# Moving the third group's decay scans behind two mask operations on the vector engine

## The chip, the cores and the metric

One core of a Trainium2 chip runs the whole kernel. The metric is the device time of the program in microseconds (us), as the median of several runs. The engines are TensorE (PE in the rows: matmuls, and PEld its weight loads), VectorE (DVE), ScalarE (ACT), GpSimd (POOL) and SyncE (SP, which issues the transfers).

## What is computed

Two stages. The first is a linear recurrence over 768 time steps, for 32 pairs of batch and head, with a 40 x 40 state each:

```python
for t in range(S):
    y[:, :, t] = np.einsum('bhd,bhde->bhe', rt, state)
    Sa = np.einsum('bhde,bhe->bhd', state, at)
    state_decay = state * wt[:, :, None, :] - np.einsum('bhd,bhe->bhde', Sa, bt)
    state = state_decay + np.einsum('bhd,bhe->bhde', vt, kt)
```

The second stage takes the recurrence's output as a (4, 768, 320) tensor and runs four gated causal attention experts over it. The change touches only the first stage.

## The kernel before

The recurrence is cut into 24 chunks of 32 time steps, and these into 6 groups `W` = 0 to 5 of four chunks. For each group there is preparation, in two halves `a` = 0 and 1:

- `a` (L192): a suffix scan of the decays `w` on DVE, which writes `SUF`; `b` (L194, L195): a reciprocal into `D1P` and the chunk's total decay `PC`; `s` (L197): the prefix scan, which writes `SC`. `SC` needs `D1P` of the same half.
- `X` (L201): two products on POOL, `AB` = `EA` times `SC`. `K` and `H` (L205): two products each on POOL, which scale the keys `KB` by `SUF`.
- `f` and `g` (L189): checks of the decays' size on ACT.
- `m` (L226): 64 small matmuls per half, of `KB` with `AB`, into PSUM `pk`; DVE and POOL read them out as `GB` and `GK`. `L`, `t`, `T`, `P`, `B`, `D`, `Q`: the group's 32 x 32 triangular inverses.

The main loop takes steps `n` = 0 to 24. The table `MAIN` gives the parts of a step their order, ten places counted from 0: `g` of chunk n (L328, reads the state `ST` and `AB`), `f` of chunk n-1 (L342 on PE, then the mask multiplication of `FX` on DVE, L343), `t`, `u` (L333), `y` of chunk n-1 (L353 reads `FX`), `z`, `k` (L310), `s` (L373 on PE, then the new state `ST` on DVE; at a group's last chunk it is L364, L364 and L378, which multiply by `PC`), `w`, `v` (L324).

The work of the groups is hung between these places by strings, one for each step: `SIDE` for a group in general, `SIDE1` for group 1, with the parts of a string split at "/" standing behind places 0, 1, 2 and so on. Group `W` prepares itself in steps 4(W-1)-4 to 4(W-1)+3, so the third group, `W` = 2, has its string -2 in step 2, its -1 in step 3 and its 0 in step 4 (the third, fourth and fifth step). The kernel writes its order by hand: each engine executes its instructions in the order in which these parts were called, and waits on semaphores for what they read and for the buffers that they overwrite.

```python
    -2: "//l2/////l30f0g/0a0b0s",
    -1: "0X0K0H/1a1b/1e/////1K1H/1f1g1s1X",
    0: "///m0//////m1L",
```

Of the kernel before, what the change touches and what calls it, by code (L numbers as in the profile page):

```python
# [35 lines left out]
         (1, "0e0l0u1l1u1w1e"), (0, "o0"), (1, "0a0b0K0H"), (0, "i1 L B k0 x3 j47 t28 j0 j23 S o1 Z"), (1, "0f0g1f1g"), (0, "D"), (1, "0s1a0X1H"),  # L36
         (0, "P v0 Q"), (1, "1b1s"))

SIDE1 = ("////////n01p1xi0o0", "///n1i1o1L//Bt6//t8", "/t8//t6////T", "//P/D/////Q")


def layouts(r, k, v, w, a, b):
# [40 lines left out]
def recurrence(tc, ctx, I, xT, FL, CM, early, tail=None):  # L83
# [4 lines left out]
    V, A, T, PL, SY = nc.vector, nc.scalar, nc.tensor, nc.gpsimd, nc.sync  # L88
# [300 lines left out]
    def at(n, s, *fs):  # L389
        jobs.setdefault((n, s), []).extend(fs)  # L390

    def items(W, line, inv, td):

        fs, i = [], 0
        while i < len(line):
            x = line[i]
            if x == " ":
                i += 1
            elif x in "LTSZPQBD":
                fs.append(inv[x])  # L400
                i += 1
            elif x in "tj":
                j = i + 1
                while j < len(line) and line[j].isdigit():
                    j += 1
                m = int(line[i + 1:j])
                if x == "t":
                    fs += td[:m]
                    del td[:m]
                else:  # L410
                    fs.append(lambda m=m: busy(m))
                i = j
            else:
                y = line[i + 1]
                if x == "x":
                    fs.append(lambda y=y: fill(int(y)))
                elif x == "l":
                    fs.append(lambda y=y: load_k(W, int(y)))
                elif x == "c":
                    fs += [lambda k=k, y=y: load_c(int(y), k) for k in (range(4) if y == '0' else (1,))]  # L420
                elif x == "m":
                    fs.append(lambda y=y: mm(W, int(y)))
                elif x in "nio":
                    fs.append(lambda x=x, y=y: mm(W, int(y), x))
                elif x == "v":
                    fs.append(lambda y=y: units[int(y)]["v"]())
                elif x == "k":
                    fs.append(lambda y=y: keys(int(y)))
                else:
                    fs.append(preps[W, int(x)][y])  # L430
                i += 2
        return fs

    preps = {(w, a): prep(w, a) for w in range(NW) for a in range(2)}
    for W in range(1, NW):
        inv = invert(W)
        td = list(inv["t"])
        for r, line in SIDE.items():
            n = 4 * (W - 1) + r
            line = SIDE1[r] if W == 1 and r >= 0 else line  # L440
            for k, part in enumerate(line.split("/") if n >= 0 else ""):
                assert k < 10
                at(n, k, *items(W, part, inv, td))
        assert not td
# [406 lines left out]
def body(tc, I, out):  # L851
    with ExitStack() as ctx:
        dp = ctx.enter_context(tc.tile_pool(name="xd", bufs=1, space=DRAM))
        xT = dp.tile([4, 320, 768], F32, name="xT")
        fp = ctx.enter_context(tc.tile_pool(name="flag", bufs=1))
        FL = fp.tile([128, 24], F32, name="FL")
        CM = fp.tile([128, 261], F32, name="CM")
        FI = fp.tile([1, 1], I32, name="FI")
        with ExitStack() as c1:
            c1.enter_context(tc.manual_schedule())  # L860
            pre = []
            def tail(raw):
                p, jobs = prepare(tc.nc, ctx.enter_context(tc.tile_pool(name="pre", bufs=1, side="right", reuse_waits="tile")), I, xT, raw)
                pre.append(p)
                return jobs
            recurrence(tc, c1, I, xT, FL, CM, ExitStack(), tail)
        with ExitStack() as c2:
            moe(tc, c2, I, xT, out, CM[:, 0:128], pre[0], FL, FI)

        far = tc.nc.values_load(FI, min_val=0, max_val=1)  # L870
        with tc.If(far != 0):
            with ExitStack() as c3:
                c3.enter_context(tc.manual_schedule())
                step_by_step(tc, c3, I["RAW"], xT)
            with ExitStack() as c4:
                moe(tc, c4, I, xT, out, CM[:, 0:128], pre[0])
# [25 lines left out]
```

## Time and profile before

| | us |
|---|---|
| median of 3 runs | 609.68 |
| lowest, highest of them | 608.61, 610.55 |
| the profiled execution's own time | 608.79 |
| its span, first to last instruction | 607.0 |
| PE busy in the span | 566.0 (93%) |
| DVE busy | 475.9 (78%) |
| ACT busy | 364.2 (60%) |
| POOL busy | 257.3 (42%) |

The recurrence takes the first 345 us or so. The busy shares are means over two stages with different limits, so the place of the change has to be read by itself: steps 2 to 4 lie between 72 and 116 us.

### The profile page before, as it was taken

What the parts mean: (1) busy time and instruction counts of PE and PEld (TensorE: products, weight loads), DVE (VectorE), ACT (ScalarE), POOL (GpSimd) and SP (SyncE); (2) the same over time, 40 slices, a digit from 0 to 9 for tenths busy, and PEclk for the clock granted to TensorE, in tenths of its full rate; (3) what the DMA queues carried; (4) which work ended last, traced back from release to release, by engine and by line L of the source; (5) the groups of instructions that cost most, each with busy time, mean ns of one, the idle gap of its engine ahead of it and who ended that gap; (6) DMA issues with size and microseconds to landing.
All of it is one profiled execution on the core that took longest, in us unless ns stands there. A gap on an engine that the chain in (4) does not pass through costs nothing.

```text
span 607.0 us, 23642 instructions
## 1 busy us (share of the span) xinstructions
PE 566.0 (93%) x10111; PEld 496.1 (82%) x10111; DVE 475.9 (78%) x963; ACT 364.2 (60%) x740; POOL 257.3 (42%) x233
## 2 busy tenths in 40 slices
PE   7998999899999999999999879989999989999996
PEld 3547898899989989989999768878888878987884
DVE  8999899589498678766324369999989997898892
ACT  4854356367356456644546337757776777778873
POOL 5247309807914931960000232546544353333550
PEclk9999999999999999999999879989999999999998
DMA  6622352453354255223146244212311312020102
GB/s 153 176 89 57 119 150 69 119 143 117 94 162 123 78 145 148 67 71 97 49 138 159 55 115 117 53 50 68 84 43 45 82 36 70 24 53 11 56 2 72
DMA packets 44196, 54.09 MB, mean 89 GB/s; under 512 B 20098, under 2 KB 33666, under 8 KB 44082
## 3 DMA queue, kind: packets, MB, share of 16 engines
q1 hardware_dynamic: 43794, 52.32, 31.0%
q8 instruction: 82, 1.34, 0.9%
q10 hardware_dynamic: 288, 0.17, 0.2%
q14 instruction: 32, 0.26, 0.1%
HBM read 38.31 MB, written 7.86 MB: 76 GB/s over the span
## 4 chain that ended last, share of the span: by engine, by line
PE 60%; DVE 22%; DMA 6%; ACT 5%; issue 3%; POOL 2%; SPq 0%; DVEq 0%; ACTq 0%
PE pt L659 6%; PE ot L784 4%; PE pk L272 4%; PE sc L739 4%; PE ps L373 4%; PE pf L353 4%; PE pt L769 4%; PE pt L795 4%; PE pf L355 3%; PE pk L226 3%; PE pg L324 3%; PE pu L333 3%; PE pk L310 3%; PE pg L328 3%; PE pf L342 2%
## 5 line engine op out<-in xcount | busy, mean ns | idle before, releaser
L761 POOL TENSOR_TENSOR P<-P,m 128x128 f32<-128x128 f32 (+2 forms) x96 | 89.1, 950 | 116.5 <-DVE m L757 59.5
L201 POOL TENSOR_TENSOR AB<-EA,SC 40x1024 f32<-40x1024 f32 x18 | 48.9, 2714 | 83.5 <-PE pg L328 61.6
L750 ACT ACTIVATE P<-sc,m 128x128 f32<-128x128 f32 (+2 forms) x96 | 60.8, 634 | 25.5 <-DVE m L749 15.0
L784 PE MATMUL ot<-pt,vv 128*128 128x256 f32 (+1 forms) x384 | 61.1, 292 | 5.7 <-DVE ots L790 5.5
L739 PE MATMUL sc<-ks,qs 128*128 128x384 f32 (+4 forms) x256 | 62.3, 346 | 3.6 <-ACT P L750 2.9
L773 DVE TENSOR_TENSOR pt<-pt,pt 128x384 fp32r<-128x384 f32 (+1 forms) x96 | 59.0, 619 | 5.3 <-ACT pt L772 3.6
L784 PEld LDWEIGHTS ot<-pt,vv 128*128 128x128 f32 x384 | 51.5, 191 | 9.8 <-DVE ots L790 8.2
L749 DVE TENSOR_REDUCE m<-sc 128x1 f32<-128x128 f32 (+2 forms) x96 | 58.7, 615 | 0.9 <-PE sc L742 0.4
L772 ACT ACTIVATE pt<-pt 128x384 fp32r<-128x384 f32 (+1 forms) x96 | 51.9, 543 | 10.5 <-PE pt L769 9.0
L205 POOL TENSOR_TENSOR KB<-KB,SUF 104x512 f32<-104x512 f32 x38 | 57.0, 1534 | 0.9 <-DMA KB<-in_EK 0.5
L769 PE MATMUL pt<-CM,P 128*128 128x128 f32 x336 | 53.0, 275 | 3.8 <-DVE qs L668 2.6
L353 PE MATMUL pf<-FX,LS 128*40 128x64 f32 x768 | 47.7, 224 | 3.6 <-DVE FX L343 3.4
L353 PEld LDWEIGHTS pf<-FX,LS 128*40 128x40 f32 x768 | 42.3, 118 | 6.6 <-DVE FX L343 5.5
L659 PE MATMUL pt<-xh,wq 128*128 128x384 f32 x192 | 42.9, 359 | 4.7 <-DVE qs L668 4.5
L739 PEld LDWEIGHTS sc<-ks,qs 128*128 128x128 f32 x256 | 40.4, 191 | 7.4 <-ACT P L750 6.9
L355 PE MATMUL pf<-RX,SD 80*40 80x64 f32 x736 | 45.8, 222 | 0.0
L233 POOL TENSOR_TENSOR GK<-GK,CM 128x512 f32<-128x512 f32 x23 | 27.5, 1196 | 41.0 <-DVE GK L231 29.8
L335 ACT ACTIVATE R<-pu 32x640 f32<-32x640 f32 x48 | 33.3, 694 | 19.1 <-PE pu L333 18.5
L330 ACT ACTIVATE GT<-pg,CM 128x320 f32<-128x320 f32 x48 | 22.7, 523 | 36.3 <-PE pg L328 36.1
L343 DVE TENSOR_TENSOR FX<-pf,MK 128x1024 f32<-128x1024 f32 x24 | 29.1, 1213 | 18.6 <-PE pf L342 18.5
L769 PEld LDWEIGHTS pt<-CM,P 128*128 128x128 f32 x336 | 36.7, 141 | 7.4 <-issue 3.4
L355 PEld LDWEIGHTS pf<-RX,SD 80*40 80x40 f32 x736 | 41.6, 119 | 0.2 <-ACT SD L350 0.2
(152 smaller groups left out, 1367.4 us busy)
## 6 DMA issues: line engine op xcount, KB each, us to landing
ks<-ks SPq DMA_DIRECT2D x32, 192.0 KB
KB<-in_EK SPq DMA_DIRECT2D x32, 160.0 KB
EA<-in_EA SPq DMA_DIRECT2D x24, 160.0 KB
V<-in_V SPq DMA_DIRECT2D x24, 160.0 KB
R<-in_VX SPq DMA_DIRECT2D x48, 80.0 KB
RX<-in_RX SPq DMA_DIRECT2D x48, 80.0 KB
RB<-in_RB SPq DMA_DIRECT2D x48, 80.0 KB
xT<-XT SPq DMA_DIRECT2D x24, 160.0 KB
```

Of the source, the lines that this page charges most:

```text
L205: e.tensor_tensor(x, x, sv[:, :, 1:33].rearrange("p (x t c) n -> p x t c n", t=2, c=4)[:, :, t], op=OP.mult)
L353: T.matmul(pf[rows(r), x], ls[:, x, r], FX[:, :, x, r], start=True, stop=c == 0)
L355: T.matmul(pf[rows(r), x], SD[:, x, r], RX[:, :, x, r], start=False, stop=True)
L659: T.matmul(p, w, x, start=(j == 0), stop=(j == len(prs) - 1))
L739: T.matmul(ps[:, c, 0:cw], QS[b][:, e, o], KS[b][:, e, z, k], start=(z == 0), stop=(z == 1 and not last), skip_group_check=True)
L749: V.tensor_reduce(m[:, 0, t:t + 1], ps[:, 0:ch, 0:cw], axis=AX.XY, op=OP.max, negate=True)
L750: later(DE, lambda: A.activation(pv, ps[:, 0:ch, 0:cw], AF.Exp, bias=m[:, 0, t:t + 1], accum_out=m[:, 1, t:t + 1]))
L761: PL.tensor_tensor(P[:, 0:n], P[:, 0:n], m[:, 3, t:t + 1].to_broadcast([128, n]), op=OP.mult)
L769: T.transpose(p[:, 128 * y:128 * y + 128], st["P"][t][:, 128 * c:128 * c + 128], ident)
L772: A.activation(h, p[:, 0:n], AF.Copy)
L773: later(DL, lambda: V.tensor_tensor(l, p[:, 0:n], f32(h), op=OP.subtract))
L784: T.matmul(po[:, 128:256] if one else po, VV[b][:, k, e].rearrange("p a b -> p (a b)"), PT[:, 256 * k:256 * k + (128 if one else 256)], st ...
```

## The change

A second table of exceptions, `SIDE2`, gives group 2 strings of its own for steps 2, 3 and 4; `SIDE1` becomes a dictionary with the same content. The two scans of half 0 (`0a0b0s`) leave the end of step 2 (behind place 8) for step 3, behind place 1, that is behind the mask of `FX`; `0X0K0H` are written behind them instead of behind place 0. The last scan `1s` and the product `1X` leave the end of step 3 for step 4, behind place 1, again behind a mask of `FX`; `1K1H` are written at the end of step 3 instead of behind its place 7.

```diff
-SIDE1 = ("////////n01p1xi0o0", "///n1i1o1L//Bt6//t8", "/t8//t6////T", "//P/D/////Q")
+SIDE1 = {0: "////////n01p1xi0o0", 1: "///n1i1o1L//Bt6//t8", 2: "/t8//t6////T", 3: "//P/D/////Q"}
+
+SIDE2 = {-2: "//l2/////l30f0g", -1: "/0a0b0s0X0K0H1a1b/1e//////1f1g/1K1H", 0: "/1s1X//m0//////m1L"}
...
-            line = SIDE1[r] if W == 1 and r >= 0 else line
+            line = {1: SIDE1, 2: SIDE2}.get(W, {}).get(r, line)
```

On DVE, where step 2 ends and step 3 begins, before (`DD` is the last transpose of group 1's inverse, `SUF_86`, `D1P` and `SC_100` are half 0 of the third group, `SUF_87` its half 1; the lines are those of the kernel before):

```order
L259 STREAM_TRANSPOSE DD_90<-MT_89 128x16x32
L192 SCALAR_TENSOR_TENSOR SUF_86<-EW_84,D_83 104x1056
L194 RECIPROCAL D1P_88<-SUF_86 104x8
L195 TENSOR_TENSOR PC_97<-SUF_86 104x8
L197 SCALAR_TENSOR_TENSOR SC_100<-EW_84,D1P_88 104x1056
L343 TENSOR_TENSOR FX_117<-pf,MK 128x1024
L192 SCALAR_TENSOR_TENSOR SUF_87<-EW_85,D_83 104x1056
```

The same place of the changed kernel, whose lines below the tables are numbered higher by two:

```order
L261 STREAM_TRANSPOSE DD_90<-MT_89 128x16x32
L345 TENSOR_TENSOR FX_117<-pf,MK 128x1024
L194 SCALAR_TENSOR_TENSOR SUF_86<-EW_84,D_83 104x1056
L196 RECIPROCAL D1P_88<-SUF_86 104x8
L197 TENSOR_TENSOR PC_97<-SUF_86 104x8
L199 SCALAR_TENSOR_TENSOR SC_100<-EW_84,D1P_88 104x1056
L194 SCALAR_TENSOR_TENSOR SUF_87<-EW_85,D_83 104x1056
```

The mask has moved ahead of half 0's four instructions, and half 1's suffix scan now follows half 0's prefix scan directly.

On DVE, where step 3 ends and step 4 begins, before (`ps` is the state's update, `TT_110` the inverse that `u` reads, `pk` the result of `m0`):

```order
L364 TENSOR_TENSOR ps<-ps,PC_96 104x2x320
L378 TENSOR_TENSOR ST_118<-ST_118,ps 104x640
L281 TENSOR_TENSOR TT_110<-TT_110,pk 48x32x16 x2
L197 SCALAR_TENSOR_TENSOR SC_100<-EW_85,D1P_88 104x1056
L343 TENSOR_TENSOR FX_117<-pf,MK 128x1024
L229 TENSOR_TENSOR GB_105<-pk,CM 128x512
```

And in the changed kernel:

```order
L366 TENSOR_TENSOR ps<-ps,PC_96 104x2x320
L380 TENSOR_TENSOR ST_118<-ST_118,ps 104x640
L283 TENSOR_TENSOR TT_110<-TT_110,pk 48x32x16 x2
L345 TENSOR_TENSOR FX_117<-pf,MK 128x1024
L199 SCALAR_TENSOR_TENSOR SC_100<-EW_85,D1P_88 104x1056
L231 TENSOR_TENSOR GB_105<-pk,CM 128x512
```

Here the mask and half 1's prefix scan have changed places, and nothing else. On PE, ACT, POOL and SP the order of all instructions is the same in both kernels: the parts that were written elsewhere keep their rank among their engine's instructions.

## Rows read from the trace of the kernel before

**Rows 1.** Who waited for whom, PE, 60 to 122 us: total, times, longest

```profile
PE pk L226 <- POOL AB L201: 1.2, 1, 1.2
PE pf L353 <- DVE FX L343: 1.2, 2, 0.6
PE pg L328 <- DVE ST L380: 0.8, 1, 0.8
```

**Rows 2.** Timeline, PE, step 3: start, duration, engine line, [idle before <-releaser]

```profile
85.54 1.15 PE L342 MATMUL pf<-RB,VR 80*64 80x64 f32 x32 [0.17 <-ACT VR L339]
...
90.44 1.30 PE L333 MATMUL pu<-GT,TT 64*32 64x80 f32 x32
92.39 0.36 PE L353 MATMUL pf<-FX,LS 128*40 128x64 f32 x3 [0.65 <-DVE FX L343]
```

**Rows 3.** Timeline, DVE, steps 3 and 4

```profile
85.41 1.03 DVE L259 STREAM_TRANSPOSE DD<-MT 128x512 f32<-128x512 f32 x1
86.28 2.30 DVE L192 TENSOR_TENSOR_SCAN SUF<-EW,D 104x1056 f32<-104x1056 f32 x1
...
88.86 2.36 DVE L197 TENSOR_TENSOR_SCAN SC<-EW,D1P 104x1056 f32<-104x1056 f32 x1
91.13 1.20 DVE L343 TENSOR_TENSOR FX<-pf,MK 128x1024 f32<-128x1024 f32 x1
92.25 3.48 DVE L192 TENSOR_TENSOR_SCAN SUF<-EW,D 104x1056 f32<-104x1056 f32 x1
...
95.88 1.84 DVE L195 TENSOR_TENSOR PC<-SUF 104x8 f32<-104x8 f32 x1
...
99.83 0.82 DVE L378 TENSOR_TENSOR ST<-ST,ps 104x640 f32<-104x640 f32 x1
100.57 1.40 DVE L281 TENSOR_TENSOR TT<-TT,pk 48x512 f32<-48x512 f32 x2
102.00 3.18 DVE L197 TENSOR_TENSOR_SCAN SC<-EW,D1P 104x1056 f32<-104x1056 f32 x1
105.21 1.23 DVE L343 TENSOR_TENSOR FX<-pf,MK 128x1024 f32<-128x1024 f32 x1
```

**Rows 4.** Timeline, POOL, the third group's products

```profile
91.35 6.34 POOL L201 TENSOR_TENSOR AB<-EA,SC 40x1024 f32<-40x1024 f32 x2 [18.84 <-DMA EA<-in_EA]
97.77 11.84 POOL L205 TENSOR_TENSOR KB<-KB,SUF 104x512 f32<-104x512 f32 x8
109.57 4.41 POOL L201 TENSOR_TENSOR AB<-EA,SC 40x1024 f32<-40x1024 f32 x2
```

**Rows 5.** Timeline, PE, step 4

```profile
101.05 1.13 PE L328 MATMUL pg<-ST,AB 104*64 104x40 f32 x32
...
105.13 2.08 PE L226 MATMUL pk<-KB,AB 104*64 104x64 f32 x64
107.05 0.31 PE L353 MATMUL pf<-FX,LS 128*40 128x64 f32 x4
...
111.66 1.13 PE L324 MATMUL pg<-V,GK 64*64 64x40 f32 x32
114.03 2.09 PE L226 MATMUL pk<-KB,AB 104*64 104x64 f32 x64 [1.24 <-POOL AB L201]
```

**Rows 6.** Timeline, POOL, the same products of the fourth group

```profile
140.78 6.39 POOL L201 TENSOR_TENSOR AB<-EA,SC 40x1024 f32<-40x1024 f32 x2 [20.53 <-PE pg L328]
...
159.10 4.44 POOL L201 TENSOR_TENSOR AB<-EA,SC 40x1024 f32<-40x1024 f32 x2
```

**Rows 7.** Timeline, second group: POOL's products, DVE's scan beside them

```profile
50.61 6.30 POOL L201 TENSOR_TENSOR AB<-EA,SC 40x1024 f32<-40x1024 f32 x2 [2.35 <-ACT MT L276]
...
50.40 2.33 DVE L192 TENSOR_TENSOR_SCAN SUF<-EW,D 104x1056 f32<-104x1056 f32 x1
```

**Rows 8.** Timeline, PE, the fourth group's last matmuls of `m`

```profile
162.60 1.13 PE L324 MATMUL pg<-V,GK 64*64 64x40 f32 x32
163.66 2.08 PE L226 MATMUL pk<-KB,AB 104*64 104x64 f32 x64
```

**Rows 9.** Stretches: us, busy of PE, PEld, DVE, ACT, POOL, granted clock, DMA

```profile
112.80:114.00 1.20, 0.00 (x0) 0.00 (x0) 0.00 (x0) 0.02 (x1) 1.18 (x1) 1.00 0.57 143
114.00:116.00 2.00, 1.97 (x68) 1.97 (x68) 0.00 (x0) 0.00 (x0) 1.86 (x2) 1.00 0.64 183
...
352.00:356.00 4.00, 0.24 (x1) 0.27 (x2) 2.22 (x5) 0.10 (x2) 1.40 (x1) 0.78 0.92 238
356.00:360.00 4.00, 4.00 (x13) 4.00 (x14) 3.37 (x19) 1.18 (x3) 2.21 (x3) 0.50 0.05 12
```

## What the change should do to the time

> **What bounds the kernel now.** PE is busy for 93% of the span, so only a place where PE stands still can give time back, or take more. I read PE's waits in the stretch of the change first [rows 1]. They name three releasers: the mask of `FX` on DVE (twice, 1.2 us together), the `AB` products of POOL (1.24 us, once) and the state. Then the timelines of PE, DVE and POOL there. In step 3, PE finishes `f` at 86.69 (85.54 + 1.15) and `u` at 91.74, and then stands for 0.65 us until the mask is done [rows 2]. The mask's input was ready at 86.69, but DVE was in the two scans of half 0 until 91.22 and wrote the mask only from 91.13 to 92.33 [rows 3]. So the scans cost PE 0.65 us, and this is what the change can give back at most in that step. The second look goes to what the scans feed. POOL starts half 0's `AB` products at 91.35, 0.13 us after `SC` is done at 91.22 [rows 3, 4]. The row names a transfer as the releaser, but the wait has several semaphores and in the fourth group the same start names PE; the scan's end is what fits the time. From there POOL runs without a pause through two products of `AB`, eight of `KB` and two of `AB`, until 113.98 [rows 4]. At 114.03 PE starts the last 64 matmuls of `m` after an idle of 1.24 us, and that is POOL's end plus 0.05 [rows 5]. The reader should see that half 0's scans begin a chain (scan, POOL for 22.63 us, PE) that already ends last in step 4. PE's wait for the mask lies beside that chain, with 1.24 us of slack behind it.
>
> **The change, part by part.** No instruction is added or removed. Only DVE's order changes, at two places; the order of PE, ACT, POOL and SP stays, and so do the transfers that SP issues.
>
> Mask ahead of half 0's scans (step 3). The mask needs `pf` at 86.69; DVE is done with the transpose ahead of it at 86.44 (85.41 + 1.03) [rows 2, 3]. It starts near 86.7 and ends near 87.9, well ahead of `u`'s end, so PE's 0.65 us go, and PE is early by 0.65 us from there. What DVE pays: the first scan began at 86.28. It will now begin one mask later, 86.7 plus 1.12 (the distance of the mask's start from the next start, 91.13 to 92.25 [rows 3]), which is 87.82. That is 1.54 us later, of which 1.12 is the mask and the rest is idle time waiting for `pf`. Bounds: if the mask's start lags the matmuls by 0.1 us it is 1.65, and if it starts at the transpose's end it is 1.3. I take 1.55. Half 0's `SC` is then ready at 92.77 and POOL starts at 92.9.
>
> The chain on POOL. Its length in the third group is 22.63 us (91.35 to 113.98 [rows 4]) and in the fourth 22.76 (140.78 to 163.54 [rows 6]), though DVE's scans meet it at other moments there. The length contains time in which POOL and DVE hold each other up: the first pair of products takes 6.34, the last pair of the same form 4.41 [rows 4], and the scan beside the first pair takes 3.48 instead of 2.30 [rows 3]. In the changed order half 1's suffix scan follows half 0's prefix scan with no mask between, and starts just ahead of POOL. The second group has this order already: the scan starts at 50.40, POOL at 50.61, the scan takes 2.33 and the pair 6.30 [rows 7]. So the pair's length stays, between 6.30 and 6.39. The other meeting, with `1s` (3.18 instead of 2.36 [rows 3]), stays inside POOL's eight `KB` products, which will run from about 99.3 to 111.1. I take 22.63 again, with 22.5 to 22.8 as bounds. POOL ends at 115.5, and PE's `m` starts at 115.6 instead of 114.03: plus 1.55 us.
>
> The Trainium skill, SBUF — State Buffer, section "Who interferes with whom", says that a VectorE instruction with two SBUF inputs and a GpSimd instruction that reads SBUF exclude each other, the one that starts first holding the shared port to its end. By that rule the scan would run from 92.7 to 95.0 and the pair behind it for 4.4 us, to 99.4, where the row's 6.34 from 92.9 gives 99.24: the sum would be plus 1.7 instead of plus 1.55, and the time 611.4.
>
> What PE does until then. If nothing else moves, PE reaches `m` at 112.79 - 0.65 = 112.1. What can make it later is the state. Half 1's `PC` was held on DVE until POOL's pair was done (95.88 + 1.84 = 97.72), and behind it in DVE's queue stand the two multiplications by `PC` and the addition that ends at 100.65; PE's `g` of step 4 starts at 101.05 with no idle [rows 3, 5]. With the pair ending 1.55 us later the addition ends between about 100.3 (if `PC` gets in between the two products) and 102.3, so `g` starts between 100.4 and 102.4, up to 1.35 later than before. PE then reaches `m` between 112.1 and 114.15. Both lie ahead of 115.6, so this costs nothing in the sum; the cover is POOL's chain.
>
> `1s` behind the mask of step 4. Before, that mask ended at 106.44 and PE began `y` at 107.05 straight from `m0` [rows 3, 5], so there is nothing to win. What waits behind `1s` now: the read-out of `m0`, which PE's `k` needs, and half 1's `AB` products. The scan will start between 103.7 and 106.8, takes 2.4 to 3.5 us and is done by 110.3, while POOL gets to those products at about 111.1. `k` may be up to 1 us late; that lies in PE's slack of at least 1.4 us ahead of `m`. Cost: 0, with 0.5 as the upper bound if every delay falls together. `1K1H`, written two places later, have the same rank on POOL: 0.
>
> After `m` everything follows PE, or starts from what PE and DVE finish, so I find nothing that takes the delay back: in the fourth group POOL's chain ends at 163.54 and PE comes to its `m` at 163.66 [rows 6, 8], both started from the shifted work.
>
> Sum: plus 1.55 us. Against the profiled execution's own time it is 608.79 + 1.55 = 610.3; that execution lies 0.9 us under the median, so against the median 609.68 it is 611.2, plus 0.25%.
>
> **The rivals.** First, the gain stays. If the suffix scan and the first pair don't hold each other up in the new order, the pair takes 4.4 instead of 6.34, POOL ends at 113.6, and PE, which is there at 112.1, starts `m` at 113.65, 0.4 us earlier: 609.3. With more saved at the second meeting it could reach the 0.65 us, 609.0. It decides by the pair's length: under 4.8 us there is a gain. For it: the length does contain some 2 us of hold-up. Against it: the second group, with this very order, shows 6.30 [rows 7].
>
> Second, no change: the delay is there at 114 us and is made up later, at the hand-over between the stages, where PE was nearly idle from 352 to 356 us [rows 9]. It would need a stop there that does not come from the recurrence's last chunks. For it only that the rows there are dense with transfers; against it that these transfers bring the recurrence's own output. 609.7.
>
> Third, slower by more. PE would stand for up to 3.5 us ahead of `m` (112.1 to 115.6) instead of 1.24. After 1.2 idle us the granted clock stayed at 1.00, but after a stretch of 4 us with PE busy for 0.24 it was 0.50, the lower level of 1.2 GHz [rows 9]. If the clock fell here too, and the 4 us behind it ran at half speed, 2 us of work would be lost: 613.2. It decides by the idle time: if `g` waits for the state, PE arrives at 114 and the idle is 1.5 us, as before. Against it: the rows on both sides of the present wait are at 1.00.
>
> The Trainium skill, TensorE: Matmul & The Clock Gate, section "What's actually happening", has the lower level as the default that activity lifts, which is the mechanism of this rival; no row here has an idle time of just this length.
>
> **How the numbers follow.** A comparison of this kernel's runs can tell about 0.3%, 1.8 us, from no change. The forecast of 611.2 gets 0.62, with its own bounds 610.7 to 611.9; about a third of that lies over 0.3%. The gain gets 0.14, no change 0.13, the clock 0.11. Slower by over 0.3%: 0.62 / 3 + 0.11 = 0.32. Faster by over 0.3% needs more than any row offers; 0.06 for what I don't see. Within 0.3%: 0.62. The range of 609.2 to 612.6 leaves out most of the clock's case and part of the gain's.
>
> **What would show it.** Right: the mask of step 3 starts near 86.7 and PE has no wait for it; POOL's first pair starts near 92.9 and takes 6.3; PE's wait for `AB` ahead of `m` grows from 1.24 to between 1.4 and 3.5; `m` starts near 115.6, and all later rows are 1.5 us later. Wrong: a pair of 4.4 us, `m` at 114.0 or earlier, a granted clock under 1.00 after it, or a later stretch in which the difference shrinks. If half 0's scans start at 86.3 as before, the change did not do what it says.

## The result: slower by 0.6%

| | median, us | against the kernel before |
|---|---|---|
| before | 608.5 (20 runs) | |
| changed | 612.14 (20 runs) | 1.0059, 95% interval 1.004 to 1.0078 |

That is 3.6 us more, with 2.4 to 4.7 as the interval. The profiled execution of the changed kernel took 609.52 us, only 0.7 us more than that of the kernel before (608.79), so the total of this one pair of profiles does not show the loss. The place of the change does.

The page of the changed kernel, its span and engines:

```profile
span 607.7 us, 23642 instructions
...
PE 565.9 (93%) x10111; PEld 496.1 (82%) x10111; DVE 475.1 (78%) x963; ACT 364.6 (60%) x740; POOL 257.5 (42%) x233
```

Who waited for whom in the changed kernel, PE, 60 to 122 us (total, times, longest), the first two rows, beside [rows 1]:

```profile
PE pk L228 <- POOL AB L203: 3.2, 1, 3.2
PE pg L330 <- DVE ST L382: 0.8, 1, 0.8
```

The wait for the mask of step 3 has left the list (so has that of step 5, 0.55 us before: PE now comes there 3 us later). The wait for POOL's products has grown from 1.2 to 3.2 us.

DVE's timeline in steps 3 and 4 (start, duration, engine, line, with the idle time ahead), beside [rows 3]:

```profile
86.95 1.23 DVE L345 TENSOR_TENSOR FX<-pf,MK 128x1024 f32<-128x1024 f32 x1 [0.28 <-PE pf L344]
88.09 2.35 DVE L194 TENSOR_TENSOR_SCAN SUF<-EW,D 104x1056 f32<-104x1056 f32 x1
...
90.71 2.36 DVE L199 TENSOR_TENSOR_SCAN SC<-EW,D1P 104x1056 f32<-104x1056 f32 x1
92.98 2.33 DVE L194 TENSOR_TENSOR_SCAN SUF<-EW,D 104x1056 f32<-104x1056 f32 x1
...
95.47 1.85 DVE L197 TENSOR_TENSOR PC<-SUF 104x8 f32<-104x8 f32 x1
97.25 0.81 DVE L366 TENSOR_TENSOR ST<-ST,PC 104x640 f32<-104x640 f32 x1
...
99.44 0.82 DVE L380 TENSOR_TENSOR ST<-ST,ps 104x640 f32<-104x640 f32 x1
...
104.24 2.81 DVE L199 TENSOR_TENSOR_SCAN SC<-EW,D1P 104x1056 f32<-104x1056 f32 x1
```

POOL's timeline, the third group's products, beside [rows 4]:

```profile
93.20 6.91 POOL L203 TENSOR_TENSOR AB<-EA,SC 40x1024 f32<-40x1024 f32 x2 [20.45 <-DMA EA<-in_EA]
100.19 11.29 POOL L207 TENSOR_TENSOR KB<-KB,SUF 104x512 f32<-104x512 f32 x8
111.44 4.39 POOL L203 TENSOR_TENSOR AB<-EA,SC 40x1024 f32<-40x1024 f32 x2
```

The chain runs from 93.20 to 115.83. That is 22.63 us, to the hundredth what it was, and it starts 1.85 us later. This execution is 0.21 us late already at `k` of step 2, so the change's own share is 1.64 us.

PE's timeline in steps 4 and 5, beside [rows 5]:

```profile
100.96 1.13 PE L330 MATMUL pg<-ST,AB 104*64 104x40 f32 x32
...
111.58 1.13 PE L326 MATMUL pg<-V,GK 64*64 64x40 f32 x32
115.89 3.21 PE L228 MATMUL pk<-KB,AB 104*64 104x64 f32 x64 [3.18 <-POOL AB L203]
118.88 1.56 PE L330 MATMUL pg<-ST,AB 104*64 104x40 f32 x32
```

PE is at `m` at 112.71 (112.79 before; 0.29 us earlier, counted from `k` of step 2), stands for 3.18 us, and then needs 3.21 us for the 64 matmuls that took 2.09. The stretches around it say why (length, then busy time of PE, PEld, DVE, ACT and POOL, granted clock, DMA):

```profile
112.80:114.00 1.20, 0.00 (x0) 0.00 (x0) 0.00 (x0) 0.00 (x0) 1.12 (x2) 1.00 0.62 154
114.00:115.80 1.80, 0.00 (x0) 0.00 (x0) 0.00 (x0) 0.00 (x0) 1.80 (x1) 1.00 0.60 189
115.80:119.80 4.00, 3.91 (x82) 3.91 (x84) 0.59 (x1) 0.00 (x0) 2.23 (x3) 0.59 0.14 40
119.80:121.80 2.00, 2.00 (x56) 1.93 (x54) 2.00 (x3) 0.95 (x2) 1.13 (x1) 0.97 0.04 8
```

Behind the wait the clock is granted at 0.59 for 4 us, which is mostly the lower level of 1.2 GHz, and it is back at 0.97 in the next two. In the kernel before, the 1.24 us of idle time were followed by 1.00 [rows 9].

I measure the whole stretch by the start of `k`, from step 2 (ahead of the change) to step 5 (behind it). In the kernel before:

```profile
80.50 0.93 PE L310 MATMUL pk<-CM,KB 104*128 104x104 f32 x8
...
122.65 0.93 PE L310 MATMUL pk<-CM,KB 104*128 104x104 f32 x8
```

and in the changed kernel:

```profile
80.71 0.93 PE L312 MATMUL pk<-CM,KB 104*128 104x104 f32 x8
...
125.64 0.93 PE L312 MATMUL pk<-CM,KB 104*128 104x104 f32 x8
```

42.15 us become 44.93, so the stretch is 2.78 us longer. The steps behind it keep that delay; at the recurrence's last `k` it is 2.90. It shrinks only at the hand-over between the stages, where the clocks of the two executions differ. The stretch of the hand-over in the kernel before:

```profile
330.00:345.00 15.00, 12.82 (x306) 11.61 (x302) 6.04 (x9) 5.34 (x8) 3.97 (x12) 0.89 0.16 45
```

and in the changed kernel:

```profile
330.00:345.00 15.00, 13.28 (x340) 11.90 (x340) 8.11 (x11) 8.24 (x12) 3.98 (x12) 1.00 0.28 69
```

Where the clock stays at 1.00 there, 1.3 us of the delay at the last `k` is gone at the first matmuls of the second stage. This is so in both profiles of the changed kernel, and in four experiments below, `fill`, `fill_again`, `delay` and `late_all`; `last_only`, `late_before` and `late_after` have 0.89 to 0.92 there and gain nothing. So it comes with the change and without it, and what decides it is not shown. The profiles give part of the loss back at this place; the medians, 3.6 us apart, show that executions in general do not. It is why one profile's total was worth less than its middle.

### The profile page after: what moved, and what is told of

Same layout as the page of the kernel before. It is cut to its first block, busy times and chain, and to the rows that moved or that the text cites. A ratio compares the mean times of both kernels' runs of the same rounds, so it can differ in the third digit from the quotient of the medians.

```text
span 607.7 us, 23642 instructions
## 1 busy us (share of the span) xinstructions
PE 565.9 (93%) x10111; PEld 496.1 (82%) x10111; DVE 475.1 (78%) x963; ACT 364.6 (60%) x740; POOL 257.5 (42%) x233
## 4 chain that ended last, share of the span: by engine, by line
PE 59%; DVE 20%; DMA 7%; ACT 6%; issue 4%; POOL 2%; SPq 0%; ACTq 0%; DVEq 0%
PE pk L274 5%; PE pt L661 5%; PE ps L375 4%; PE ot L786 4%; PE pf L355 4%; PE sc L741 4%; PE pt L797 4%; PE pf L357 3%; PE pt L771 3%; PE pk L228 3%; PE pu L335 3%; PE pg L326 3%; PE pk L312 3%; PE pg L330 3%; PE pf L344 3%
## 5 line engine op out<-in xcount | busy, mean ns | idle before, releaser
L355 PE MATMUL pf<-FX,LS 128*40 128x64 f32 x768 | 46.2, 220 | 2.5 <-DVE FX L345 1.6
L355 PEld LDWEIGHTS pf<-FX,LS 128*40 128x40 f32 x768 | 40.6, 115 | 5.4 <-DVE FX L345 4.2
L357 PE MATMUL pf<-RX,SD 80*40 80x64 f32 x736 | 44.4, 218 | 0.1
L357 PEld LDWEIGHTS pf<-RX,SD 80*40 80x40 f32 x736 | 40.0, 116 | 0.2 <-ACT SD L352 0.2
```

What stands on the lines that cost most here:

```text
L355: T.matmul(pf[rows(r), x], ls[:, x, r], FX[:, :, x, r], start=True, stop=c == 0)
L357: T.matmul(pf[rows(r), x], SD[:, x, r], RX[:, :, x, r], start=False, stop=True)
```

## The experiments

Theory A, from the result: the loss has two terms. POOL's chain starts one mask later and ends last at `m`, some 1.6 us; and PE's longer idle time ahead of `m` lowers its clock, another 1.1 us or more. Theory B: the last scan's new place, or something else in DVE's new order, costs. In the first table the stretch is from `k` of step 2 to `k` of step 5, against 42.15 us in the kernel before. Each ratio is to the runs of the kernel before on the same chip.

| kernel | stretch | ratio | 95% interval |
|---|---|---|---|
| changed | +2.78 | 1.0059 | 1.004 to 1.0078 |
| `first_only` | +1.80 | 1.0022 | 1.0005 to 1.004 |
| `last_only` | +0.03 | 1.001 | 0.9986 to 1.0034 |
| `delay` | +1.64 | 1.0042 | 1.0018 to 1.0065 |
| `fill` | +1.65 | 1.0024 | 1.0002 to 1.0046 |
| `after_again` | +2.99 | 1.0074 | 1.0046 to 1.0102 |
| `fill_again` | +1.67 | 1.0005 | 0.9985 to 1.0025 |

### One half of the change at a time

The first half alone (half 0's scans behind the mask of step 3):

```diff
+SIDE2 = {-2: "//l2/////l30f0g", -1: "/0a0b0s0X0K0H1a1b/1e/////1K1H/1f1g1s1X"}
```

> Only the first half of the change: half 0's scans and products behind the mask of step 3; the last scan and its product stay where they were, at the end of step 3. Theory A (the chain from half 0's scans over POOL to PE's last matmuls of m is one mask late, and the longer idle there lowers PE's clock): POOL's first pair starts 1.6 to 1.9 us later than before, PE waits about 3.2 us for AB instead of 1.24, the matmuls of m take about 3.2 us at the lower clock instead of 2.09, step 5 is about 3 us later, and the ratio to before is like the whole change's, 1.004 to 1.008. Theory B (the last scan's new place costs, by holding up POOL's products in step 4): POOL's chain is as long as before and PE's wait stays near 1.2 us plus 1.5, with a ratio of 1.000 to 1.003.

PE's timeline in step 4, the two groups of `m`, and the clock from 108 to 112 us:

```profile
105.25 0.33 PE L228 MATMUL pk<-KB,AB 104*64 104x64 f32 x2 [1.15 <-POOL KB L207]
106.38 2.82 PE L228 MATMUL pk<-KB,AB 104*64 104x64 f32 x61 [0.80 <-POOL KB L207]
...
115.51 2.09 PE L228 MATMUL pk<-KB,AB 104*64 104x64 f32 x64
```

```profile
108.00:112.00 4.00, 4.00 (x90) 3.92 (x87) 1.43 (x3) 0.00 (x0) 4.00 (x4) 0.66 0.01 4
```

The expectation was half wrong. POOL's chain is late as in the whole change (its end is at 115.34, where this execution's `k` of step 2 is 0.31 us early), but PE pays elsewhere. With `1s` still ahead of the mask, that scan (101.07 to 104.23) now meets the third of the eight `KB` products, one of half 0's four, which takes 3.22 us instead of some 1.2. `m0` waits for these, 1.15 and 0.80 us, and runs at a lower clock. PE comes to the last matmuls of `m` so late that there is no wait left: its work ahead of them ends at 115.58, POOL's chain at 115.34. The stretch is 1.80 us longer, little more than POOL's delay of 1.67, because the earlier stops were for the most part paid out of PE's slack. The ratio, 1.0022, lies in the range of theory B, but not by its mechanism, since the last scan was not moved here. So the second half of the change does something: it keeps the first half from stopping `m0`. In the changed kernel `1s` starts at 104.24 and holds up the fifth product, one of half 1's. By doing so the second half gathers PE's idle time into one piece.

The second half alone:

```diff
+SIDE2 = {-1: "0X0K0H/1a1b/1e//////1f1g/1K1H", 0: "/1s1X//m0//////m1L"}
```

> Only the second half of the change: the last scan and its product behind the mask of step 4, half 0's scans as before. Theory A: POOL's chain starts at 91.3 as before and keeps its length of 22.6 us, PE waits 1.2 us for AB, the matmuls of m take 2.1 us at full clock, ratio 0.998 to 1.001. Theory B: POOL's chain ends later by 1 us or more and the ratio is 1.003 or more.

PE's wait ahead of `m`, and POOL's chain:

```profile
114.36 2.08 PE L228 MATMUL pk<-KB,AB 104*64 104x64 f32 x64 [1.24 <-POOL AB L203]
```

```profile
91.67 6.37 POOL L203 TENSOR_TENSOR AB<-EA,SC 40x1024 f32<-40x1024 f32 x2 [18.83 <-DMA EA<-in_EA]
98.11 11.82 POOL L207 TENSOR_TENSOR KB<-KB,SUF 104x512 f32<-104x512 f32 x8
109.90 4.41 POOL L203 TENSOR_TENSOR AB<-EA,SC 40x1024 f32<-40x1024 f32 x2
```

The wait is 1.24 us, the chain 22.64, the stretch +0.03. The scan's new place costs nothing by itself, as theory A had it; the ratio alone, with its interval of half a per cent, could not have said so.

### POOL late, DVE as before

Ten unread memsets on POOL between half 0's first products and the rest, in the order of the kernel before:

```diff
+SIDE2 = {-1: "0XN00K0H/1a1b/1e/////1K1H/1f1g1s1X"}
...
+    DUM = ring("DUM", [128, 64], 1)[0]
...
+                elif x == "N":
+                    fs += [lambda: PL.memset(DUM, 0.0)] * 10
```

> The order of the kernel before on every engine, plus ten memsets of a 128 x 64 tile that nobody reads on POOL, between half 0's first products and the rest, some 1.6 us in all. Theory A: a late POOL chain alone is enough for the loss. DVE's order and PE's wait for the mask in step 3 (0.65 us) stay as before, POOL ends its chain 1.5 to 1.8 us later, PE waits 2.7 to 3.1 us for AB, step 5 is 1.6 us late, and 1.3 us more if the clock falls; ratio 1.002 to 1.008. If it is something else in DVE's new order that costs, PE's wait grows by less than 0.5 us and the ratio stays within 1.000 to 1.002.

POOL's timeline, and PE's two groups of `m`:

```profile
93.13 6.36 POOL L204 TENSOR_TENSOR AB<-EA,SC 40x1024 f32<-40x1024 f32 x2 [18.84 <-DMA EA<-in_EA]
99.55 2.03 POOL L423 MEMSET DUM<- 128x64 f32 x10
101.72 11.28 POOL L208 TENSOR_TENSOR KB<-KB,SUF 104x512 f32<-104x512 f32 x8
112.95 4.42 POOL L204 TENSOR_TENSOR AB<-EA,SC 40x1024 f32<-40x1024 f32 x2
```

```profile
107.30 0.33 PE L229 MATMUL pk<-KB,AB 104*64 104x64 f32 x2 [0.32 <-POOL KB L208]
108.44 2.02 PE L229 MATMUL pk<-KB,AB 104*64 104x64 f32 x61 [0.81 <-POOL KB L208]
...
117.42 2.08 PE L229 MATMUL pk<-KB,AB 104*64 104x64 f32 x64 [1.36 <-POOL AB L204]
```

The memsets took 2.03 us and the chain's end moved by 1.6. The idle time came in two pieces, 1.1 us at `m0` and 1.36 at `m`, not in one of 2.7 to 3.1 as expected. The stretch grew by 1.64 us. So a late POOL is enough for the first term of theory A, with DVE's order untouched and the clock at 1.00. The ratio of 1.0042 stands for 2.6 us, more than this profile's stretch shows.

### The clock

The whole change, with 13 unread products on PE in the wait ahead of `m`:

```diff
-SIDE2 = {-2: "//l2/////l30f0g", -1: "/0a0b0s0X0K0H1a1b/1e//////1f1g/1K1H", 0: "/1s1X//m0//////m1L"}
+SIDE2 = {-2: "//l2/////l30f0g", -1: "/0a0b0s0X0K0H1a1b/1e//////1f1g/1K1H", 0: "/1s1X//m0//////j13m1L"}
```

> The whole change, plus 13 products of 128 x 512 bf16 on PE with a result that nobody reads, ahead of the last matmuls of m in step 4, so that PE is busy for some 2.8 of the 3.2 us in which it waits for POOL. Theory A with the clock as the second term: m starts at the same time as in the changed kernel, near 115.9, but takes 2.1 us instead of 3.2, the granted clock stays at 1.00 from 112 to 120 us, the delay of step 5 shrinks from about 3.0 to about 1.7 us, and the ratio falls to 1.002 to 1.004. If the clock has nothing to do with PE's idle time, m takes 3.2 us again and the ratio stays at 1.004 to 1.008.

PE's timeline, and the stretches from 116 to 120 us:

```profile
113.12 2.98 PE L174 MATMUL pf<-D 104*128 104x512 bf16 x13
116.58 2.09 PE L228 MATMUL pk<-KB,AB 104*64 104x64 f32 x64 [0.48 <-POOL AB L203]
```

```profile
116.00:118.00 2.00, 1.51 (x49) 1.42 (x50) 0.00 (x0) 0.00 (x0) 1.84 (x3) 1.00 0.49 141
118.00:120.00 2.00, 2.00 (x76) 2.00 (x73) 1.21 (x2) 0.31 (x1) 0.89 (x1) 1.00 0.00 0
```

`m` still waits for POOL, but takes 2.09 us, the clock stays at 1.00, and the stretch is 1.65 us longer instead of 2.78. Work for nothing made the kernel faster. To have both kernels in one comparison, each ran once more:

> The changed kernel once more, beside the fill on the same chip. Theory A: in its profile PE waits 3.2 us for AB, the clock falls behind that wait, and step 5 is 2.8 us later than before, counted from step 2; ratio 1.004 to 1.007.

> The changed kernel with the 13 unread products on PE in the wait, beside the changed kernel. If the clock's fall is the second term of the loss, it is 1 to 2.5 us (0.2 to 0.4%) faster than the changed kernel in the same comparison, at a ratio of 1.002 to 1.004. If the first comparison's difference was chance, the two lie within 0.1%.

The changed kernel showed the same again: PE at `m`, and its clock from 118 to 120 us,

```profile
116.80 3.44 PE L228 MATMUL pk<-KB,AB 104*64 104x64 f32 x64 [3.37 <-POOL AB L203]
```

```profile
118.00:120.00 2.00, 2.00 (x43) 2.00 (x42) 0.00 (x0) 0.00 (x0) 1.09 (x1) 0.50 0.00 0
```

and a stretch of +2.99, against +1.67 with the fill. The medians were 612.87 (6 runs) and 608.95 (11 runs). That is 3.9 us apart, more than the 1 to 2.5 expected and more than the 1.3 us of the profiles; their intervals (1.0046 to 1.0102, and 0.9985 to 1.0025) don't overlap. The ratio with the fill, 1.0005, is under the 1.002 to 1.004 that was expected: in the medians of this comparison the filled kernel can't be told from the kernel before, though its stretch is 1.67 us longer. The median of the granted clock over the span was 0.98 for the changed kernel in these runs and 0.989 with the fill. So the clock's share is 1.1 to 1.3 us in the profiles that I can look into, and may be larger in other executions.

### Taking the wait away

If the loss is the wait at `m`, it must go when `m` has other work ahead of it. Here the third group's last matmuls of `m` stand behind `g`, `f` and `t` of step 5, without the change and with it:

```diff
+SIDE2 = {0: "///m0", 1: "//m1Lt6/B/////t8", 2: "/t14T////////P"}
```

> The kernel before with one difference: the third group's last matmuls of m and the start of its inverse stand behind g, f and t of step 5 instead of at the end of step 4 (the inverse's small steps are spread as 6, 8 and 14 over steps 5 and 6, so that the state isn't held up). Theory A (POOL's chain ends last at m): PE has 3 us of other work ahead of m, its wait of 1.24 us goes, and the mask of step 5, which stood behind the inverse's transpose, comes earlier too; 1.2 to 1.8 us less, ratio 0.997 to 0.999. If the wait was not what bounds this place, the time stays: 0.999 to 1.001.

```diff
+SIDE2 = {-2: "//l2/////l30f0g", -1: "/0a0b0s0X0K0H1a1b/1e//////1f1g/1K1H", 0: "/1s1X//m0", 1: "//m1Lt6/B/////t8", 2: "/t14T////////P"}
```

> The changed kernel with the same difference as late_before. Theory A: the loss of the change was the wait at m and the clock that fell behind it. With m behind 3 us of other work, POOL's end at 115.8 is no longer waited for (0.3 us at most), the clock stays at 1.00 and the change shows the 0.65 us that it saves at the mask of step 3, or less: ratio to before 0.996 to 0.999, and within 0.2% of late_before. If the change costs by something else than this wait, the kernel is still 0.3% or more slower than late_before.

`m` in `late_before`, then in `late_after`:

```profile
116.37 2.09 PE L228 MATMUL pk<-KB,AB 104*64 104x64 f32 x64
```

```profile
117.30 2.08 PE L228 MATMUL pk<-KB,AB 104*64 104x64 f32 x64 [0.56 <-POOL AB L203]
```

| kernel | `k` of step 2 to `k` of step 7 | ratio | 95% interval |
|---|---|---|---|
| before | 64.79 us | | |
| `late_before` | -1.19 | 0.9987 | 0.9964 to 1.001 |
| `late_after` | -1.07 | 0.9979 | 0.9956 to 1.0002 |

With `m` there, the change costs 0.12 us in this stretch, not 2.78, and it has no measurable effect on the time. PE is 0.79 us earlier at `k` of step 3, loses part of that again, and 0.56 at POOL's end. This is the test that decides: the same new order of masks and scans costs 0.6% or nothing that can be measured, depending on what PE does while POOL is late. The gain of 1.1 to 1.2 us itself does not last: at `k` of step 9 both kernels stand 0.1 to 0.2 us behind the kernel before. In the fourth group `m` stands where it was, and PE, now early, waits 0.9 us there for POOL's products, which it did not before.

A second way to shorten the chain, half 1's `AB` products on DVE instead of POOL:

```diff
+SIDE2 = {-1: "0X0K0H/1a1b/1e/////1K1H/1f1g1s", 0: "///m01x//////m1L"}
```

> The kernel before, with half 1's two AB products done on DVE behind the read-out of m0 in step 4 instead of on POOL at the chain's end (4.4 us there). Theory A: the chain then ends near 112.0, before PE gets to m at 112.8, and PE's wait of 1.24 us goes; ratio 0.997 to 0.999. If the chain's length does not matter, the ratio is 0.999 to 1.001, and it is over 1.001 if the products hold up DVE's state in step 4.

DVE's timeline, and PE's wait:

```profile
109.34 5.24 DVE L203 TENSOR_TENSOR AB<-EA,SC 40x1024 f32<-40x1024 f32 x2
```

```profile
114.73 2.09 PE L228 MATMUL pk<-KB,AB 104*64 104x64 f32 x64 [1.17 <-DVE AB L203]
```

A miss. In the second group of the kernel before, where POOL is done by then, the two products take 2.44 us on DVE:

```profile
62.30 2.44 DVE L201 TENSOR_TENSOR AB<-EA,SC 40x1024 f32<-40x1024 f32 x2
```

Here, beside the last of POOL's `KB` products and its read-out of `GK`, they take 5.24. PE's wait only changed its name; the ratio is 0.9991 (0.9968 to 1.0014).

### A faster version

`late_before` for groups 2 to 5 alike:

```diff
-    0: "///m0//////m1L",
-    1: "/t16//B/////t12",
-    2: "/T////////P",
+    0: "///m0",
+    1: "//m1Lt6/B/////t8",
+    2: "/t14T////////P",
```

> As late_before, for groups 2 to 5 alike. In groups 3 to 5 PE comes to m within 0.1 us of POOL's end in the kernel before, so there is no wait for AB to win, but the mask of the step behind it stands behind the inverse's transpose in each group (0.6 us each). Theory A: 0.4 to 0.6 us per group more than late_before, ratio 0.995 to 0.998. If the later inverse is waited for in the step behind, it is slower than late_before.

> The kernel before with the last matmuls of m behind g, f and t in groups 2 to 5, beside the next kernel. Theory A: ratio 0.996 to 0.999 as before.

> The same with the change under study added for the third group. Theory A: PE's 0.65 us at the mask of step 3 are saved, and 0.3 to 0.6 us of them are lost again to a wait for POOL's end ahead of m; within 0.1% of the kernel without it (ratio 0.996 to 0.999). If the change costs by itself, it is 0.3% or more slower than that.

`late_all` came to 0.9968 (0.9946 to 0.999) and again to 0.9948 (0.9927 to 0.997), some 2 to 3 us faster than the kernel before and faster than the changed one. With the change under study added (group 2's strings as in `late_after`) it was 0.9981 (0.9958 to 1.0005). In the stretch up to step 7 the two differ by 0.09 us (-1.18 and -1.09), in the medians by 1.2 us or 0.2% (605.39 and 606.61), between the 0.1% and the 0.3% of the expectation, and the intervals overlap. Whether the change still costs something there is open; no gain from it shows.

## Why the prediction was right, and where its size was wrong

**The direction and the range.** The forecast was slower, 611.2, with a range of 609.2 to 612.6; the median is 612.14. But the likeliest case was plus 0.25%, and the measured interval starts at plus 0.4%. "Slower by over 0.3%" had 0.32 of the chance and "within 0.3%" 0.62. That the median lies in the range is in part luck. The range was laid around 609.68, the median of three runs, and over 20 runs the kernel before has 608.5. As a difference the forecast was plus 1.55 us in a range of minus 0.5 to plus 2.9. The measured plus 3.6 (2.4 to 4.7) is over twice the forecast and outside that range, though its interval reaches into it.

**The mask.** Right in its time and its wait: it started at 86.95 (86.7 expected, and 0.21 of it is the late execution), and PE's wait for it went. What PE gained by it was not 0.65 us. In six other profiles with this order PE is 0.77 to 0.79 us early at `k` of step 3. In the first profile of the changed kernel it is only 0.29, because `u` stopped behind its first matmul:

```profile
90.66 0.25 PE L335 MATMUL pu<-GT,TT 64*32 64x80 f32 x1
91.15 1.29 PE L335 MATMUL pu<-GT,TT 64*32 64x80 f32 x31 [0.24 <-issue]
```

The profile names no releaser for this stop. `late_before`, with the old order of DVE, has it too (0.26 us), so the change is not its cause.

**The scans' delay.** 1.55 us expected; POOL starts 1.64 us later in the first profile, and the stretch with the clock kept up (`fill`, `fill_again`) gives 1.65 and 1.67. The idle time ahead of the mask, 0.28 us, is in line with that.

**The chain's length.** 22.63 expected, 22.63 measured, by other parts than I said. The first pair of products took 6.91, not 6.30 to 6.39, and the eight products behind it 11.29 instead of 11.84. That the sum came out to the hundredth is luck. The pair is longer because `PC` and the first multiplication by it got in between its two products (95.47 + 1.85 = 97.32, and the next row starts at 97.25); in the kernel before, that multiplication met the first `KB` product instead (1.74 us, 1.19 in the changed kernel), so what POOL lost in the pair it did not lose later. The Trainium skill, SBUF — State Buffer, section "Who interferes with whom", calls the port that VectorE and GpSimd share an exclusive lock. By that rule the prediction had plus 1.7 for the sum, where the row gave 1.55. The measured 1.64 to 1.67 does not decide between the two: it is the scans' delay, and the chain kept the row's length. The single rows agree with the rule. Half 1's suffix scan, which started 0.22 us ahead of the pair, took 2.33 us; before, it started 0.90 us behind the pair and took 3.48. `PC`, 0.12 us in half 0, took 1.85 beside the pair. `last_on_dve` agrees as well, since products moved from POOL to DVE shortened nothing there.

**The state.** The earlier of the two branches came true: `PC` got in between the products, the state was done at 100.26 and `g` started at 100.96 without a stop. This is the branch with the longest idle time at `m`.

**`1s` behind the mask of step 4.** Right: nothing was expected of it, and `last_only` shows 0.03 us.

**The slack ahead of `m`: the term that was mis-sized.** I wrote that PE comes to `m` between 112.1 and 114.15, "both lie ahead of 115.6, so this costs nothing in the sum". It did cost: the idle time of 3.18 us was followed by the lower clock, 1.1 us in the first profile and 1.3 in the second. PE itself lost 1.5 us: from the start of `m` to that of `f` in step 5 it needs 4.37 us in both profiles, 2.82 in the kernel before; the shorter wait for step 5's mask covers the rest. I had this as the third rival, at 2 us and with a chance of 0.11, and it was the one that came true, on top of the forecast. Its 613.2 is plus 3.5 us as a difference, and 3.6 was measured. The reason that I gave against it, that the rows on both sides of the present wait are at 1.00, was a row of an idle time of 1.24 us; the rival was about one of up to 3.5. My own sum made the idle time longer, and the clock should have been a term in it.

**What is left.** The stretches are 2.8 and 3.0 us longer, the medians say 3.6 (2.4 to 4.7) and 4.5 (2.8 to 6.2 from its interval). The intervals hold the stretches. But the profiles give 1.3 us back at the hand-over, and both profiled executions are among the fastest of their kernel: 609.52 is the fourth of 20, 611.08 the first of 6. So what a usual execution loses beyond them stands in no trace. Among the 20 runs the time goes with the granted clock over the span, from 608.69 us at 0.992 to 615.26 at 0.972, which points at the clock; where it was lower is not shown. With the fill the ratio is 1.0024 and 1.0005 although POOL is as late, so the greater part of the loss hangs on PE's idle time at `m`.

**No change, made up later.** It did not happen in the recurrence: the delay at `k` of step 7 is still 2.78. At the hand-over it came true in part in the profiles, by 1.3 us, as shown above; the medians speak against it as the rule.

## What to carry to other kernels

Before moving work behind the operation that an engine waits for, ask what else starts from the moved work: 0.65 us of PE's wait were bought with a later start of a 22.6 us chain that ended last. Slack on the busiest engine is not free when the change makes it longer, because idle time on TensorE can cost clock behind it (here 3.18 us were followed by 0.59 over 4 us); price the idle time that the new order makes, not the one in the trace of before. Where two orders fight over one wait, look for other work that the waiting engine can do first: in the third group that made the fight pointless, and in groups 2 to 5 together it made the kernel 0.3 to 0.5% faster.

## What was not expected of the hardware

One idle time of 3.18 us on PE was followed by a granted clock of 0.59 over 4 us. In `delay` the idle time was 2.5 us in two pieces, 1.1 us at `m0` and 1.36 at `m`, and the matmuls behind the second piece took 2.08 us, at full clock. In `first_only` two pieces close together, 1.15 and 0.80 us with two matmuls between, were enough for 0.66 over 4 us. At the end of the recurrence PE waits 1.2 and then 0.5 us in both kernels, 2 us of matmuls apart; the clock over 330 to 345 us was 0.89 in the kernel before and 1.00 in the changed one. So the length of an idle time alone does not say whether the clock falls. And 13 products whose result nobody reads, 2.98 us of PE's time, made the changed kernel 1.1 to 1.3 us faster in that stretch, and its median 3.9 us lower.
